# Output weights ahead of group 3, the first outputs inside the second tile, and 64-token blocks from group 3 on, in a fused attention and feed-forward kernel

## The chip, the cores and the metric

The kernel runs on one core of a Trainium2 chip. Its time is the device time of one execution in microseconds (us). An execution is called slow when it is over 1.5% above the fastest of its kernel in the same call; comparisons use the fast ones. "Clock" is the mean clock that TensorE was granted in an execution, as a share of full speed.

## The reference

Linear attention with a decay per head over 4 batches, 8 heads, 768 tokens and head size 64 gives x of 3072 x 512, and a gated feed-forward layer follows. The attention goes in blocks and carries a state:

```python
for b in range(nb):                                  # blocks of 64 tokens
    intra = einsum('bhic,bhjc->bhij', qb, kb) * Dmask    # within the block
    intra = einsum('bhij,bhjd->bhid', intra, vb)
    inter = einsum('bhid,bhde->bhie', qb * lam_pow, kv_state)
    out[:, :, sl] = intra + inter
    kv_state = lam_block * kv_state + einsum('bhsd,bhse->bhde', kb * rev_pow, vb)
# x = out, tokens in rows
g = x @ w_gate
out = (g * sigmoid(g) * (x @ w_val)) @ w_out         # 512 -> 1536 -> 512
```

## The kernel before

Twelve *groups* of attention (256 tokens of one batch each) feed six feed-forward *tiles* of 512 tokens, two groups to a tile. TensorE works through the tiles' steps; the attention of coming groups is put between steps by a plan. A tile has 12 steps (gate and value matmuls of 128 of the 1536 features) and 4 output blocks of 128 tokens. Tile 1 runs in half steps of 256 tokens, 12 for group 2's tokens and 12 for group 3's.

A group has this life: k, q, v are loaded; ScalarE casts k, VectorE scales q, GpSimd scales v; k and q are transposed (groups 0 to 2 on TensorE, from 3 on by a DMA); TensorE computes the state's updates and the scores; GpSimd adds the updates to the state; TensorE computes the state's part of the output, then the part within the block. Groups below `NAT0` go in blocks of 128 tokens, the others in blocks of 64 with smaller matmuls and more states:

```python
    NAT0 = 6
    def load_fp32(g, eng, src, what, h0=0, h1=H):
        ...
        if g < NAT0:                                   # one transfer, pieces of 2*D floats = 512 B
            eng.dma_start(out=t[:, h0:h1], in_=gsrc(src, g, h0)[:, 0:h1 - h0])
            return
        ...
        parts = [(0, 128, False)] if what == "v" else [(0, M, False), (M, M, True)]
        for s in range(2):                             # 2 transfers for v, 4 for k, 4 for q
            for p0, n, rev in parts:
                eng.dma_start(...)                     # pieces of D floats = 256 B

    def cast_scaled(g, eng=nc.vector):
        ...
        nc.scalar.copy(out=..., in_=...kraw...)        # k to bf16, ScalarE
        eng.tensor_tensor(out=..., in0=...qraw..., in1=qfac(g), op=ALU.mult)   # q, VectorE
        dma_transpose(g)                               # issued by SyncE

    def ahead(g):                                      # updates, state, scores
        upd(g); scores(g)

    def core_a(g):
        inter(g, True)                                 # the state's part
        guard(g)                                       # ScalarE reads one column, orders what follows

    def core_b(g, ...):
        run_later(len(later)); intra(g, False); evac(g, fns)

    def attend(g):                                     # one merged visit for g and g + 1
        core_a(g)
        upd_mm(g + 1); upd_copy(g + 1); scores(g + 1)
        core_b(g)
        state(g + 1)                                   # (cut: bounds and masks put off)
```

and the part of the plan in question (`s1a`, `s1b`: half steps of tile 1; `sn`: steps of tile t; `wo_cast`: the cast of one piece of the output weights, on GpSimd unless an engine is named, `ACTC` is ScalarE and `DVEC` VectorE):

```python
    at(s0[5], load_group, 3)
    at(s0["11b"], cast_scaled, 3, nc.gpsimd)
    ...
    at(s1a[3], cast_scaled, 4)
    at(s1a[3], load_group, 5)
    for c in range(0, FC, 2): at(s1a[3], wo_piece, c, c + 2)     # output weights, 3.1 MB
    ...                                                # group 3 in four visits, steps 7 to 10
    at(s1b[6], ahead, 4)
    at(s1b[8], wo_cast, ACTC)
    at(s1b[9], core_a, 4); at(s1b[10], core_b, 4)
    at(s1b[11], ...)                                   # 4 outputs of tile 0, group 5 between them
    # tile 2: outputs of tile 1 at steps 0, 3, 7, 9; ahead(6) at 2, attend(6) at 6, attend(7) at 10
```

Of the kernel before, what the change touches and what calls it, by code (L numbers as in the profile page):

```python
# [14 lines left out]
def bap(t: bass.AP, ap_dims, extra_offset=0) -> bass.AP:  # L15
    return bass.AP(tensor=t.tensor, offset=t.offset + extra_offset,
                   ap=[list(t.ap[0])] + [list(d) for d in ap_dims])
# [20 lines left out]
def _body(ctx, tc, nc, q, k, v, lam, moe_w_gate, moe_w_val, moe_w_out, out):  # L38
# [7 lines left out]
    FC = DFF // 128  # L46
# [6 lines left out]



    NAT0 = 6
    NB = 4
    PB = B // 2
    groups = [(t % PB * 2 + j, t // PB) for t in range(NG // 2) for j in range(2)]
# [25 lines left out]
    def gsrc(t, g, h0):  # L85
        b, i = groups[g]
        return bass.AP(tensor=t.tensor,
                       offset=t.offset + b * H * S * D + i * 2 * BLK * D + h0 * S * D,
                       ap=[[2 * D, 2 * M], [S * D, H - h0], [1, 2 * D]])

    st = {}

    def load_fp32(g, eng, src, what, h0=0, h1=H):
# [3 lines left out]
        t = st[(what, g)]  # L97
        if g < NAT0:
            eng.dma_start(out=t[:, h0:h1], in_=gsrc(src, g, h0)[:, 0:h1 - h0])  # L99
# [87 lines left out]
    def vfac(g, h0, h1):  # L187
        return bap(dec, [[8, h1 - h0], [1, 2], [0, D]], 8 * h0 + (0 if g < NAT0 else 4))

    def qfac(g):  # L190
        return bap(dec, [[8, H], [1, 2], [0, D]], 2) if g < NAT0 else bap(qdn, [[2, H], [1, 2], [0, D]])

# [116 lines left out]
    def scores(g, cs=(0, 1), warm=0):  # L309
        if g >= NAT0:  # L310
            scores_n(g)
# [55 lines left out]
    def upd_mm(g, up=None):  # L367
# [4 lines left out]
        for s in range(2):  # L372
            for hp in range(HP):
                for r in range(2):
                    if g >= NAT0 and i == NG // B - 1 and 2 * s + r == 3:
                        continue
                    for h2 in range(2):
                        ps = slice(r * M, r * M + M)
                        h = 2 * hp + h2
                        if g >= NAT0 and r:  # L380
                            h = H - 1 - h
# [9 lines left out]
    def upd_copy(g, parts=(0, 1)):  # L391
        b, i = groups[g]
        up = st[("up", g)]
        hd = "p (h d) -> p h d"
        if i == 0 and 0 in parts:
            kv = kv_pool.tile([128, HP, D], BF16, name="kvn", tag="kvn1", bufs=2)
            nc.scalar.copy(out=kv, in_=up[0][:, 0:HP * D].rearrange(hd, h=HP))
            st[("kv", g)] = [None, kv]
        if 1 not in parts:
            return  # L400
        src = []
        for r in range(2):
            n = HP * D if g < NAT0 or (r == 1 and i == NG // B - 1) else 2 * HP * D
            u = kv_pool.tile([128, 2 * HP * D], FP32, name="ups", tag="ups", bufs=4)
            nc.scalar.copy(out=u[:, 0:n], in_=up[r][:, 0:n])  # L405
            src += [(r, u, HP * D * j) for j in range(n // (HP * D))]

        st[("ups", g)] = [u[:, o:o + HP * D].rearrange(hd, h=HP)
                          for r, u, o in sorted(src, key=lambda x: (x[2], x[0]))]
# [29 lines left out]
    def phase(g, first, rs):  # L439
        hps = range(HP) if first else range(HP - 1, -1, -1)  # L440
        return [(hp, s, r, h2) for hp in hps for s in ((0, 1) if first else (1, 0))
                for h2 in range(2) for r in rs]
# [5 lines left out]
    def cols(g, hp, s):  # L448
        return slice((hp * 2 + s) * M, (hp * 2 + s) * M + M) if g >= NAT0 else slice(hp * BLK, hp * BLK + BLK)

    def inter(g, first):
        b, i = groups[g]
        tt, op = st[("qkt", g)], st[("op", g)]
        kv = st[("kv", g)] if ("kv", g) in st else [kv0[b][i % 2]]
        started = set()
        for hp, s, r, h2 in phase(g, first, (1,) if i == 0 else (0, 1) if first else (1, 0)):
            if g < NAT0 and s:
                continue
            n = 2 * s + r if g >= NAT0 else r
            row, hq = (1 - h2, HP - 1 - hp) if g >= NAT0 and r else (h2, hp)  # L460
            dp, rm = slice(row * 64, row * 64 + 64), slice(r * M, r * M + M)
            nc.tensor.matmul(op[r][h2 * 64:h2 * 64 + 64, cols(g, hp, s)], kv[n][dp, hp],  # L462
                             tt[dp, 1, s, hq, rm] if g >= NAT0 else tt[dp, 1, :, hp, rm],
                             start=(first and (r, h2) not in started), stop=(not first),
                             skip_group_check=True)
            started.add((r, h2))

    def intra(g, first):
        b, i = groups[g]
        op = st[("op", g)]  # L470
        ssb, v_s = st[("ssb", g)], st[("vs", g)]
        started = set()
        for hp, s, r, h2 in phase(g, first, (0, 1) if first else (1, 0)):
            ps = slice(r * M, r * M + M)
            nc.tensor.matmul(op[r][h2 * 64:h2 * 64 + 64, cols(g, hp, s)],  # L475
                             v_s[ps, 2 * hp + h2, s],
                             ssb[ps, h2, hp * 2 + s] if g >= NAT0 else ssb[ps, h2, hp, s],
                             start=((first or (i == 0 and r == 0)) and (r, h2) not in started),
                             stop=(not first), skip_group_check=True)
            started.add((r, h2))  # L480

# [14 lines left out]
    def core_b(g, fns=(nc.scalar.copy, nc.scalar.copy)):  # L496
        run_later(len(later))
        intra(g, False)
        evac(g, fns)
# [64 lines left out]
    ACTC, DVEC = nc.scalar.copy, nc.vector.tensor_copy  # L564
    SPLIT = (DVEC, ACTC)
# [37 lines left out]
    st[("op", 0)] = [bank() for _ in range(2)]  # L603
    warm_into(st[("op", 0)][0], 3)
    intra(0, True)
    ring[0] = 4
    guard(0)
# [21 lines left out]
    st[("op", 1)] = [bank() for _ in range(2)]  # L629
    warm_into(st[("op", 1)][0], 3)  # L630
    intra(1, True)
    guard(1)
    ring[0] = 2
# [20 lines left out]
    def step(t, fc, b0=0, b1=B):  # L654
        steps.append((t, fc, b0, b1))
        return len(steps) - 1

    def at(n, fn, *a):
        plan.setdefault(n, []).append((fn, a))

    s0 = {fc: step(0, fc) for fc in range(2, FC - 1)}
# [6 lines left out]
    at(s0[4], w_cast)  # L668
    at(s0[4], state, 1)
    at(s0[4], load_group, 2, "v")  # L670
    at(s0[5], load_group, 3)
    at(s0[6], w_cast)
    at(s0[7], load_group, 4, "kq")
    at(s0[7], cast_half, 2, 0, (ACTC, POOLC))
    at(s0[7], cast_half, 2, 1, (ACTC, POOLC))
    at(s0[8], pe_transpose, 2, 0)
# [5 lines left out]
    at(s0[10], upd_mm, 2)  # L682
    at(s0[10], upd_copy, 2)
    at(s0["11a"], core, 2, SPLIT)
    at(s0["11b"], cast_scaled, 3, nc.gpsimd)
    at(s0["11b"], v_scale, 3, nc.gpsimd)
    at(s0["11b"], state, 2)
    at(s0["11b"], load_group, 4, "v")

    s1a = [step(1, fc, 0, 2) for fc in range(FC)]  # L690
    s1b = [step(1, fc, 2, 4) for fc in range(FC)]
    at(s1a[3], cast_scaled, 4)
    at(s1a[3], load_group, 5)
    for c in range(0, FC, 2):
        at(s1a[3], wo_piece, c, c + 2)
    at(s1a[7], scores, 3, (0,))
    at(s1a[7], run_later, 2)
    at(s1a[8], scores, 3, (1,))
    at(s1a[8], upd_mm, 3)
    at(s1a[8], run_later, 2)  # L700
    at(s1a[8], upd_copy, 3)
    at(s1a[9], core_a, 3)
    at(s1a[10], core_b, 3, SPLIT)
    at(s1a[10], v_scale, 4, nc.gpsimd)
    at(s1a[10], state, 3)
    at(s1b[3], cast_scaled, 5)
    at(s1b[3], load_group, 6)
    at(s1b[4], wo_cast)
    at(s1b[4], wo_cast)
    at(s1b[6], ahead, 4)  # L710
    at(s1b[6], run_later, 2)
    at(s1b[6], wo_cast)
    at(s1b[6], wo_cast)
    at(s1b[6], v_scale, 5, nc.gpsimd)
    at(s1b[8], wo_cast, ACTC)
    at(s1b[8], wo_cast)
    at(s1b[9], core_a, 4)
    at(s1b[10], core_b, 4)
    at(s1b[11], ffn_out, 0, 0)
    at(s1b[11], ahead, 5)  # L720
    at(s1b[11], run_later, 3)
    at(s1b[11], ffn_out, 0, 1)
    at(s1b[11], core_a, 5)
    at(s1b[11], ffn_out, 0, 2)
    at(s1b[11], core_b, 5)
    at(s1b[11], cast_scaled, 6)
    at(s1b[11], load_group, 7)
    at(s1b[11], v_scale, 6, nc.gpsimd)
    at(s1b[11], ffn_out, 0, 3)

    outs = [(1, b) for b in range(4)]
    for t in range(2, NG // 2):
        sn = [step(t, fc) for fc in range(FC)]
        if t == 2:
            at(sn[2], ahead, 6)
        for j, g in ((3 if t == 2 else 0, 2 * t + 3), (7 if t == 2 else 6, 2 * t + 4)):
            if g < NG:
                at(sn[j], cast_scaled, g)
                if g + 1 < NG:
                    at(sn[j], load_group, g + 1)  # L740
                at(sn[1 + j], v_scale, g, nc.gpsimd)
        if t + 1 < NG // 2:
            at(sn[6 if t == 2 else 4], attend, 2 * t + 2)
            at(sn[10], attend, 2 * t + 3)
        for n, o in zip((0, 3, 7, 9), outs):
            at(sn[n], ffn_out, *o)
        outs = [(t, b) for b in range(4)]
# [41 lines left out]
```

## Time and profile before

| | before |
|---|---|
| time, median of 3 | 230.56 us (227.83 to 231.1) |
| profiled execution | span 227.1 us, clock 1.000 |
| TensorE busy | 218.5 us, 96% |
| ScalarE, VectorE, GpSimd busy | 47%, 40%, 39% |
| packets under 512 B | 57650 of 88012 |

The busy shares are averages over the span. For a program of stages they say which engine to look at; what a wait is worth has to be read from the stretch it lies in, so the prediction goes by timelines. In all timelines below a line is: start, length, engine, source line, operation, tile written <- tiles read, count, and in brackets the engine's idle time just before and what ended it.

### The profile page before, as it was taken

What the parts mean: (1) busy time and instruction counts of PE and PEld (TensorE: products, weight loads), DVE (VectorE), ACT (ScalarE), POOL (GpSimd) and SP (SyncE); (2) the same over time, 40 slices, a digit from 0 to 9 for tenths busy, and PEclk for the clock granted to TensorE, in tenths of its full rate; (3) what the DMA queues carried; (4) which work ended last, traced back from release to release, by engine and by line L of the source; (5) the groups of instructions that cost most, each with busy time, mean ns of one, the idle gap of its engine ahead of it and who ended that gap; (6) DMA issues with size and microseconds to landing.
All of it is one profiled execution on the core that took longest, in us unless ns stands there. A gap on an engine that the chain in (4) does not pass through costs nothing.

```text
span 227.1 us, 5890 instructions
## 1 busy us (share of the span) xinstructions
PE 218.5 (96%) x2432; PEld 118.2 (52%) x2444; DVE 90.1 (40%) x154; ACT 106.5 (47%) x209; POOL 88.2 (39%) x129
## 2 busy tenths in 40 slices
PE   7889999999979999999999999999999999999994
PEld 3556455878854444454544544544544444444443
DVE  2754357685825214545352362253242123222200
ACT  5868585754652446363454463453433423322221
POOL 6476736642793312978373092092150000000000
PEclk9999999999999999999999999999999999999999
DMA  6999999899997779799877748815101101101122
GB/s 199 345 360 377 367 354 313 210 255 352 300 219 189 206 168 222 177 200 191 217 178 186 185 98 214 214 36 139 49 3 48 46 3 46 46 0 46 49 92 92
DMA packets 88012, 39.70 MB, mean 175 GB/s; under 512 B 57650, under 2 KB 83506, under 8 KB 87986
## 3 DMA queue, kind: packets, MB, share of 16 engines
q1 hardware_dynamic: 83474, 32.64, 55.2%
q10 hardware_dynamic: 4512, 6.69, 8.3%
q8 instruction: 19, 0.31, 0.5%
q14 instruction: 7, 0.06, 0.1%
HBM read 28.31 MB, written 6.29 MB: 152 GB/s over the span
## 4 chain that ended last, share of the span: by engine, by line
PE 84%; DMA 6%; SPq 5%; issue 1%; DVE 1%; ACT 1%; DVEq 0%; ACTq 0%
PE bank L539 27%; PE bank L517 25%; PE bank L524 24%; DMA woraw<-in_moe_w_out_dram 4%; DMA qraw<-in_q_dram 2%; PE bank L475 2%; SPq L99 2%; SPq L228 2%; PE bank L462 2%; PE bank L383 1%; PE bank L353 1%; PE bank L327 1%; PE bank L290 1%; DVE ssb L334 1%; PE bank L168 0%
## 5 line engine op out<-in xcount | busy, mean ns | idle before, releaser
L527 DVE TENSOR_TENSOR h<-sil,bank 128x512 bf16<-128x512 bf16 (+1 forms) x87 | 51.4, 595 | 110.7 <-PE bank L524 94.5
L517 PE MATMUL bank<-xt,wg_sb 128*128 128x512 bf16 (+1 forms) x348 | 76.7, 343 | 0.0
L524 PE MATMUL bank<-xt,wv_sb 128*128 128x512 bf16 (+1 forms) x348 | 76.5, 342 | 0.0
L521 ACT ACTIVATE sil<-bank 128x512 bf16<-128x512 f32 (+1 forms) x87 | 45.8, 528 | 43.4 <-PE bank L517 40.4
L539 PE MATMUL bank<-wo_sb,h 128*128 128x512 bf16 (+1 forms) x288 | 64.2, 370 | 0.7 <-issue 0.2
L524 PEld LDWEIGHTS <-wv_sb 128*128 128x128 bf16 x348 | 34.0, 98 | 28.3
L517 PEld LDWEIGHTS <-wg_sb 128*128 128x128 bf16 x348 | 32.2, 98 | 27.4 <-DVE xt L487 0.5
L539 PEld LDWEIGHTS <-h 128*128 128x128 bf16 x300 | 29.1, 98 | 32.4
L541 ACT COPY osb<-bank 128x512 f32<-128x512 f32 (+1 forms) x24 | 13.8, 576 | 54.9 <-PE bank L539 52.9
L239 POOL TENSOR_TENSOR v_s<-v,dec 128x1024 bf16<-128x1024 f32 (+1 forms) x14 | 23.2, 1665 | 13.9 <-DMA v<-in_v_dram 9.5
L422 POOL TENSOR_TENSOR kvf<-kvs,ups 128x256 f32<-128x256 f32 x8 | 5.8, 726 | 45.1 <-ACT ups L405 40.1
L334 DVE TENSOR_TENSOR ssb<-bank,causal 128x512 bf16<-128x512 f32 x24 | 15.5, 684 | 3.9 <-PE bank L327 3.8
L487 ACT CAST xt<-bank 128x512 bf16<-128x512 f32 x21 | 12.8, 665 | 3.1 <-PE bank L475 2.3
L422 POOL TENSOR_TENSOR kvf<-kvf,ups 128x256 f32<-128x256 f32 x16 | 13.4, 839 | 0.6
L431 POOL CAST kvn<-kvf 64x256 bf16<-64x256 f32 x24 | 11.6, 483 | 1.5
L405 ACT COPY ups<-bank 128x256 f32<-128x256 f32 (+1 forms) x24 | 9.5, 450 | 2.3 <-PE bank L383 1.4
L259 ACT CAST qk<-kraw 128x1024 bf16<-128x1024 f32 x9 | 9.4, 1043 | 0.0
L261 DVE TENSOR_TENSOR qk<-qraw,qdn 128x1024 bf16<-128x1024 f32 x6 | 7.7, 1286 | 3.7 <-DMA qraw<-in_q_dram 3.7
L475 PE MATMUL bank<-ssb,v_s 64*64 64x128 bf16 (+1 forms) x384 | 7.2, 208 | 2.0 <-ACT guard L446 1.7
L222 POOL CAST wv_sb<-wraw 128x1024 bf16<-128x1024 f32 (+1 forms) x7 | 6.4, 918 | 6.1 <-DMA wraw<-in_moe_w_val_dram 6.0
L358 DVE TENSOR_TENSOR ssb<-bank,causaln 128x512 bf16<-128x512 f32 x12 | 8.3, 688 | 1.2 <-PE bank L353 1.1
L233 POOL CAST wo_sb<-woraw 128x1024 bf16<-128x1024 f32 x5 | 5.7, 1171 | 5.3 <-DMA woraw<-in_moe_w_out_dram 5.3
(62 smaller groups left out, 115.6 us busy)
## 6 DMA issues: line engine op xcount, KB each, us to landing
out_dram<-osb ACTq DMA_DIRECT2D x23, 256.0 KB, 2.5
v<-in_v_dram SPq DMA_DIRECT2D x16, 256.0 KB, 4.2
woraw<-in_moe_w_out_dram SPq DMA_DIRECT2D x6, 512.0 KB, 7.1
kraw<-in_k_dram SPq DMA_DIRECT2D x24, 128.0 KB, 3.2
qraw<-in_q_dram SPq DMA_DIRECT2D x24, 128.0 KB, 3.8
wraw<-in_moe_w_gate_dram SPq DMA_DIRECT2D x5, 512.0 KB, 6.6
wraw<-in_moe_w_val_dram SPq DMA_DIRECT2D x5, 512.0 KB, 7.3
kraw<-in_k_dram SPq DMA_DIRECT2D x4, 512.0 KB, 6.5
```

Of the source, the lines that this page charges most:

```text
L239: eng.tensor_tensor(out=st[("vs", g)][:, h0:h1], in0=st[("v", g)][:, h0:h1].rearrange("p h (s d) -> p h s d", s=2), in1=vfac(g, h0, h1), o ...
L334: nc.vector.tensor_tensor(out=ssb[:, h2, 2 * c:2 * c + 2].rearrange("p a s n -> p a (s n)"), in0=sp[(c, h2)].rearrange("p (a x) -> p a x", ...
L422: nc.gpsimd.tensor_tensor(out=o, in0=f, in1=u, op=ALU.add)
L431: nc.gpsimd.tensor_copy(out=o[64 - h2 * 64:128 - h2 * 64], in_=f[h2 * 64:h2 * 64 + 64])
L475: nc.tensor.matmul(op[r][h2 * 64:h2 * 64 + 64, cols(g, hp, s)], v_s[ps, 2 * hp + h2, s], ssb[ps, h2, hp * 2 + s] if g >= NAT0 else ssb[ps, ...
L487: fns[r](out=xt[:, g % 2, :, r].rearrange("p h (m s) -> p h s m", s=2) if g < NAT0 else xt[:, g % 2, :, :, r * M:r * M + M], in_=op[r].rea ...
L517: nc.tensor.matmul(gp[:, 0:N], wg_sb[:, mc, fs], xt[:, b0 // 2:b1 // 2, mc].rearrange("p g b n -> p g (b n)"), start=(mc == 0), stop=(mc = ...
L521: nc.scalar.activation(sil[:, 0:N], gp[:, 0:N], AF.Silu)
L524: nc.tensor.matmul(vp[:, 0:N], wv_sb[:, mc, fs], xt[:, b0 // 2:b1 // 2, mc].rearrange("p g b n -> p g (b n)"), start=(mc == 0), stop=(mc = ...
L527: nc.vector.tensor_tensor(out=h_sb[:, fc, b0:b1].rearrange("p b n -> p (b n)"), in0=sil[:, 0:N], in1=vp[:, 0:N], op=ALU.mult)
L539: nc.tensor.matmul(ps, h_sb[:, fc, b], wo_sb[:, fc, c0:c1], start=(fc == 0), stop=(fc == FC - 1))
L541: fn(out=osb[:, c0:c1], in_=ps)
```

## The change

Intent: take TensorE work out of groups 3 to 5 (fewer, merged visits in 64-token form), and have the output weights ready early, so that no cast of them holds up ScalarE.

```diff
-    NAT0 = 6
+    NAT0 = 3
...
-        if i == 0 and 0 in parts:
+        if i == 0 and g >= NAT0:
+            st[("kv", g)] = [None]
+        elif i == 0 and 0 in parts:
... (two further conditions of the same kind in inter and intra)
-    at(s0[5], load_group, 3)
+    for c in range(0, FC, 2):
+        at(s0[5], wo_piece, c, c + 2)
-    at(s0[7], load_group, 4, "kq")
+    at(s0[7], load_group, 3)
-    at(s0["11b"], cast_scaled, 3, nc.gpsimd)
-    at(s0["11b"], v_scale, 3, nc.gpsimd)
+    at(s0["11b"], wo_cast)
... (the other five casts of output weights at s1a[1] to s1a[6])
+    at(s1a[8], ffn_out, 0, 0)
+    at(s1a[8], cast_scaled, 3)
+    at(s1a[8], load_group, 4)
+    at(s1a[8], v_scale, 3, nc.gpsimd)
+    at(s1a[8], ffn_out, 0, 1)
+    at(s1a[8], ffn_out, 0, 2)
+    at(s1a[8], ahead, 3)
+    at(s1a[8], ffn_out, 0, 3)
+    at(s1a[10], core, 3, SPLIT)
+    at(s1a[11], cast_scaled, 4)
+    at(s1a[11], load_group, 5)
+    at(s1b[5], ahead, 4)
+    at(s1b[9], cast_scaled, 5)
+    at(s1b[9], load_group, 6)
+    at(s1b[11], ffn_out, 1, 0)
+    at(s1b[11], attend, 4)
+    at(s1b[11], ffn_out, 1, 1)
+    at(s1b[11], ffn_out, 1, 2)
+    at(s1b[11], cast_scaled, 6)
+    at(s1b[11], load_group, 7)
+    at(s1b[11], core, 5)
+    at(s1b[11], ffn_out, 1, 3)
-    outs = [(1, b) for b in range(4)]
+    outs = []
... (tile 2: ahead(6) at step 1, group 7's cast at 2, attend(6) at 5, one step earlier each)
```

## The prediction

> **What bounds the kernel now.** I read the page first: busy shares, then the chain that ended last.

> ```profile
> PE 218.5 (96%) x2432; PEld 118.2 (52%) x2444; DVE 90.1 (40%) x154; ACT 106.5 (47%) x209; POOL 88.2 (39%) x129
> PE 84%; DMA 6%; SPq 5%; issue 1%; DVE 1%; ACT 1%; DVEq 0%; ACTq 0%
> ```

> TensorE is the bound, so a change gains only by giving it less work or fewer waits. The feed-forward work is fixed: a step is eight 512-column matmuls, 1.73 us, an output tile twelve, 2.59 us; six tiles of 12 steps and 4 outputs are 6 x (20.7 + 10.4) = 187 us. Of 227 us, 15 are the start and 3 the end; the remaining 22 are attention and waits. So I went to TensorE's timeline around groups 3, 4 and 5, whose form changes. The number before the brackets is a count; the bracket is idle time before the piece. Here group 4:

> ```profile
> 59.48 0.45 PE L383 MATMUL bank<-v_s,qk 64*64 64x64 bf16 x32
> ...
> 64.08 0.60 PE L524 MATMUL bank<-xt,wv_sb 128*128 128x256 bf16 x4
> 65.88 0.64 PE L475 MATMUL bank<-ssb,v_s 64*64 64x128 bf16 x32 [1.21 <-ACT guard L446]
> 66.46 0.61 PE L517 MATMUL bank<-xt,wg_sb 128*128 128x256 bf16 x4
> ```

> The 1.21 us is the largest hole after the start. ScalarE's timeline explains it:

> ```profile
> 64.45 1.04 ACT L233 CAST wo_sb<-woraw 128x1024 bf16<-128x1024 f32 x1 [2.24 <-DMA woraw<-in_moe_w_out_dram]
> ```

> A cast of output weights waited for its transfer and everything behind it on ScalarE waited too. That is what the change wants to cure.

> Next, what else a 64-token group needs. The stretches view (per-engine busy time and instructions, then clock, DMA share, GB/s) and SyncE's and GpSimd's timelines for group 7, already in the new form:

> ```profile
> 93.20:105.40 12.20, 12.15 (x178) 6.12 (x177) 5.37 (x7) 6.69 (x13) 10.07 (x16) 1.00 0.95 195
> ```

> ```profile
> 93.18 2.00 SPq L252 DMA_TRANSPOSE qkt<-qk  x1
> 95.23 2.92 SPq L106 DMA_DIRECT2D kraw<-in_k_dram  x4
> 98.19 3.50 SPq L106 DMA_DIRECT2D qraw<-in_q_dram  x4
> 101.73 1.26 SPq L106 DMA_DIRECT2D v<-in_v_dram  x2
> 105.38 2.70 SPq L252 DMA_TRANSPOSE qkt<-qk  x1
> ```

> ```profile
> 103.91 1.33 DVE L261 TENSOR_TENSOR qk<-qraw,qdn 128x1024 bf16<-128x1024 f32 x1 [1.03 <-DMA qraw<-in_q_dram]
> ```

> ```profile
> 89.05 0.73 POOL L422 TENSOR_TENSOR kvf<-kvs,ups 128x256 f32<-128x256 f32 x1 [8.87 <-ACT ups L405]
> ...
> 91.92 1.70 POOL L422 TENSOR_TENSOR kvf<-kvf,ups 128x256 f32<-128x256 f32 x1
> ...
> 96.44 1.91 POOL L239 TENSOR_TENSOR v_s<-v,dec 128x1024 bf16<-128x1024 f32 x1
> ```

> Two chains run beside TensorE. **The transfer chain**: transpose of a group, then loading of the next, scaling, its transpose. From one transpose's issue (93.18) the next q landed at 103.91, 10.7 us; with 1.33 us scaling the period is 12.2 us, with the DMA engines 95% busy. v landed 14 us after the transpose issue (107.60 in GpSimd's timeline). **The GpSimd chain**: state update (89.05 to 96.44, 7.4 us) plus v scaling 1.91 us; with 1.2 us from the update matmuls (87.84) to its start, 10.5 us from one group's update matmuls to the next group's scaled v. Before, both chains just fit: group 7's scaled v is ready at 98.35, and its update matmuls start at 98.41.

> [...] The new form reads 64 values, 256 B, per piece, the old one 512 B. The trace agrees: 195 GB/s at 95% busy above, against 371 GB/s in the stretch from 20 to 30 us, whose pieces are 512 B and longer. [...] The trace agrees: the state addition that meets the q scaling (91.73 to 93.04) took 1.70 us, the others 0.72. [...]

> **The change, part by part.** Everything up to 40.4 us (first half-width step of tile 1) stays, apart from loads: the 3.1 MB of output weights now go ahead of group 3. In the before trace each 512 KB load there takes about 1.5 us of SyncE's queue; starting at 29 the last should land near 44 (an estimate), and its cast on GpSimd ends near 46. The outputs need it at 48.3. I expect no wait for weights.

> TensorE work, from 40.4 to the start of tile 3 (114.8 before; both kernels have done the same there, since tile 1's outputs move forward). Fixed: two tiles' steps and eight outputs, 62.2 us. Attention before: 74.4 - 62.2 = 12.2 us: group 3 in four visits 2.25, group 4 3.55 with its wait, group 5 2.3, groups 6 and 7 0.75 + 1.55 + 1.4, and about 0.4 of fringe. After, without waits: group 3 0.75 + 1.25, group 4's scores 0.75, the merged visit 1.4, group 5 alone about 1.0, groups 6 and 7 0.75 + 1.4 + 1.4: about 8.9. **Saving: 3.2 us**, 1.4%. That is all there is to win; the rest of the program is the same instructions.

> What it adds: group 3 is cast only at step 9 of tile 1 instead of at 40.5, behind the copy of the first output on ScalarE, and five groups (3 to 7) plus group 8's preparation must pass both chains before tile 3. Working along (us):
> - Outputs 48.3 to 50.9. ScalarE copies 0.6, issues the store 0.4, casts k 1.04: transpose 3 is issued at 53.1 and lands 4.3 later, 57.4 (shown: 3.7 to 5.5 uncongested). TensorE reaches the scores at 56.5: **wait 0.9**.
> - Output, two steps, group 3, seven half steps of 0.87: 69.5. Transpose 4 issued at 66.0, landed 70.3: **wait 0.3**.
> - Six half steps, an output, group 4's first part: 79.0. v of group 5 lands at 66.0 + 14 = 80, scaled 81.9; q at 76.7, transpose issued 78.1, landed 82.4. **Wait 3.4**, visit over at 83.3.
> - Two outputs: 88.5. Now the guard of group 5 stands on ScalarE behind an output copy, a store issue and k's cast, 2.1 us, while TensorE has 0.4 us of work: **wait 1.9**. Group 5 over 91.4, last output 94.0, two steps 97.5, group 6's update.
> - Four steps (6.9 us, no outputs between them any more; before there was one) and 0.4 lead to group 7's update at 105.5, but the GpSimd chain gives 97.6 + 10.5 = 108.1: **wait 2.6**.
> - Five steps: 117.9, group 8's v and transpose ready near 118.9: **wait 0.6**, end 119.8, last step 121.5.

> Waits 9.7 against 3.2 saved: **+6.5 us** in the straight working. [...]

> **Rivals.** (a) Transfers are quicker than in the before trace, as tile 2 has no stores beside them: period 11 us instead of 12.2, landing 3.7. Then the waits at groups 3, 5 and 8 shrink to about 0.4, 2.2 and 0, but guard and GpSimd waits stay: +3.5 us. For it: stores took about 12% of the queues' share between 82 and 106; against: 1.5 MB in 256 B pieces is most of the load either way. (b) The chains don't bite and the intent comes out: -3 us. For it: the hole at 64 is real and visits merge. Against: GpSimd's 10.5 us is a sum of durations no reordering shortens, and before it had no slack. (c) Output weights come late because 1.5 MB more is ahead of them than I think; ScalarE would block at its third cast near 43.9 and the steps behind it, as at 64.45 before: +2 on top. Against: 5 us of margin at that cast.

> **Range and chances.** The straight working gives +6.5, rival (a) +3.5, rival (b) -3. I weigh to +5.3. The three runs before average 229.8 us (227.8 to 231.1), so I predict 235.0 us. Eight in ten between 229.5 (rival (a) on a good run, or part of (b)) and 239.0 (with (c)). Faster by over 2% would need 4.6 us and only 3.2 can be saved: 0.03. Slower by over 2% needs +4.6, under the straight working and over (a): 0.58; within 2%: 0.39.

> **What would show it.** In the changed profile: TensorE busy falls under 95%; the waits list shows update and score matmuls or their weight loads held by scaled v (GpSimd) and by transposes in groups 5 and 7, and a hole of about 2 us before group 5's second part, released by the guard; transposes from group 3 on issued every 11 to 13 us; packets under 512 B up by some 18 thousand (three groups of 1.5 MB / 256 B), which makes DMA fuller between 45 and 115; the output-weight casts no longer wait 2 us; tile 3 begins near 120 instead of 114.8, and all after it only shifts. I am wrong if tile 3 begins at 112 to 114 with no holes in tile 2 (the chains have slack I don't see), or if the loss lies before 48 us.

## The result, and the profile after

| | before | after |
|---|---|---|
| time, median of 4 | 229.38 us (227.83 to 231.1) | 242.2 us (240.44 to 243.91) |
| ratio after / before | | 1.0556 (95%: 1.0436 to 1.0677) |
| profiled execution | 227.1 us, clock 1.000 | 240.3 us, clock 0.977 |
| tile 3 begins | 114.8 us | 128.1 us |

Ratios here and below are the mean time of one kernel's fast runs over that of the other's fast runs of the same rounds, so not quite the ratio of the medians. The change is 12.8 us slower. The direction was forecast, the size not: 242.2 lies above the range.

The page of the changed kernel, its busy shares, its chain that ended last, and the granted clock in 40 slices of the span (tenths of full speed):

```profile
PE 222.3 (93%) x2492; PEld 119.1 (50%) x2492; DVE 88.2 (37%) x149; ACT 108.5 (45%) x209; POOL 94.5 (39%) x146
PEclk9999999998899979799999999999999999999999
...
PE 69%; POOL 10%; DMA 9%; issue 5%; SPq 4%; DVE 1%; ACT 1%; POOLq 0%; DVEq 0%
```

TensorE's part of the chain has fallen from 84% to 69%; GpSimd, which did not appear before, has 10%. And the clock, at its full value throughout before (1.000), dips in three places (0.977 over the span).

TensorE's timeline of the changed kernel, the pieces that follow an idle time of over half a microsecond, and the outputs (source line 543) behind some of them:

```profile
58.28 0.45 PE L353 MATMUL bank<-qkt 64*64 64x64 bf16 x32 [1.72 <-DMA qkt<-qk]
58.66 4.45 PE L543 MATMUL bank<-wo_sb,h 128*128 128x512 bf16 x12
...
73.25 0.45 PE L353 MATMUL bank<-qkt 64*64 64x64 bf16 x32 [0.66 <-DMA qkt<-qk]
...
78.88 2.75 PE L543 MATMUL bank<-wo_sb,h 128*128 128x512 bf16 x12
...
84.03 0.45 PE L383 MATMUL bank<-v_s,qk 64*64 64x64 bf16 x32 [2.02 <-POOL v_s L239]
86.64 0.64 PE L353 MATMUL bank<-qkt 64*64 64x64 bf16 x32 [2.17 <-DMA qkt<-qk]
...
87.64 6.21 PE L543 MATMUL bank<-wo_sb,h 128*128 128x512 bf16 x24
...
96.12 0.58 PE L479 MATMUL bank<-ssb,v_s 64*64 64x64 bf16 x32 [1.89 <-ACT guard L448]
96.63 4.25 PE L543 MATMUL bank<-wo_sb,h 128*128 128x512 bf16 x12
...
114.90 0.44 PE L383 MATMUL bank<-v_s,qk 64*64 64x64 bf16 x32 [2.52 <-POOL v_s L239]
```

The waits stand where the prediction put them and end as it said: transposes (DMA qkt), scaled v (GpSimd), the guard. With 0.26 us at group 8 they sum to 11.2 us (11.5 with 0.30 us at group 3's guard); predicted were 9.7. Two of them can be read to the tenth: the guard 1.89 (predicted 1.9) and group 7's updates 2.52 (2.6).

But look at the outputs: twelve matmuls of 512 columns take 2.75 us at 78.88, and 4.25 us from 96.63 on. The stretches view of the changed kernel (length, busy us and instructions of PE, PEld, DVE, ACT, POOL, then the granted clock, DMA share and GB/s), cut at the clock's changes:

```profile
55.24:58.65 3.41, 1.70 (x69) 0.88 (x67) 0.00 (x0) 1.66 (x3) 0.58 (x2) 1.00 0.88 219
58.65:62.06 3.41, 3.41 (x20) 1.18 (x10) 1.29 (x2) 0.00 (x0) 3.06 (x7) 0.51 1.06 269
82.50:85.90 3.40, 0.45 (x32) 0.33 (x31) 0.00 (x0) 1.23 (x3) 2.15 (x2) 1.00 1.00 241
85.90:89.30 3.40, 2.66 (x68) 1.52 (x69) 1.29 (x2) 1.07 (x2) 3.04 (x7) 0.52 0.71 158
```

Each pair is a stretch with a wait in it and the stretch after it: TensorE was busy 1.70 and 0.45 us of some 3.4, and for the next 3.4 us it had half its clock. A third such stretch begins at 96.3, after one with 1.5 us busy. The three together cost 1.7 + 0.9 + 1.5 = about 4.0 us: the lengths 4.45, 6.21 and 4.25 us of the outputs in them, less the 2.76, 5.35 and 2.76 us that the same outputs take at full clock in the filler run below. The prediction has no such term.

SyncE's timeline, the transposes of groups 3, 4 and 8:

```profile
53.21 1.73 SPq L252 DMA_TRANSPOSE qkt<-qk  x1
...
69.35 1.60 SPq L252 DMA_TRANSPOSE qkt<-qk  x1
...
121.92 1.61 SPq L252 DMA_TRANSPOSE qkt<-qk  x1
```

Those of groups 5, 6 and 7, cut here, are issued at 81.73, 96.03 and 109.66.

Before, the transposes of groups 3, 4 and 5 were issued at 41.6, 45.9 and 58.7, those of 6, 7 and 8 at 80.2, 93.2 and 105.4. The changed kernel starts this chain 12 us later and has not caught up at group 8, 16.5 us behind. And what was to be cured is cured. ScalarE's timeline has no wait left at its casts of output weights:

```profile
43.93 1.04 ACT L233 CAST wo_sb<-woraw 128x1024 bf16<-128x1024 f32 x1
...
45.68 1.04 ACT L233 CAST wo_sb<-woraw 128x1024 bf16<-128x1024 f32 x1
```

From tile 3 on both kernels do the same. So all of the loss arises between 40 and 128 us.

### The profile page after: what moved, and what is told of

It reads as the page before. It is cut to its first block, busy times and chain, and to the rows that moved or that the text cites. A ratio compares the mean times of both kernels' runs of the same rounds, so it can differ in the third digit from the quotient of the medians.

```text
span 240.3 us, 6057 instructions
## 1 busy us (share of the span) xinstructions
PE 222.3 (93%) x2492; PEld 119.1 (50%) x2492; DVE 88.2 (37%) x149; ACT 108.5 (45%) x209; POOL 94.5 (39%) x146
## 3 DMA queue, kind: packets, MB, share of 16 engines
q1 hardware_dynamic: 93026, 32.65, 53.1%
q10 hardware_dynamic: 4512, 6.69, 7.7%
## 4 chain that ended last, share of the span: by engine, by line
PE 69%; POOL 10%; DMA 9%; issue 5%; SPq 4%; DVE 1%; ACT 1%; POOLq 0%; DVEq 0%
PE bank L521 21%; PE bank L528 21%; PE bank L543 20%; POOL kvf L424 4%; DMA v<-in_v_dram 4%; POOL v_s L239 3%; SPq L106 2%; DMA qraw<-in_q_dram 2%; DMA qkt<-qk 2%; POOL kvn L433 2%; PE bank L479 2%; PE bank L383 1%; PE bank L466 1%; SPq L99 1%; DMA out_dram<-osb 1%
## 5 line engine op out<-in xcount | busy, mean ns | idle before, releaser
L521 PE MATMUL bank<-xt,wg_sb 128*128 128x512 bf16 (+1 forms) x348 | 76.7, 343 | 0.0
L543 PE MATMUL bank<-wo_sb,h 128*128 128x512 bf16 (+1 forms) x300 | 69.2, 387 | 0.0
L543 PEld LDWEIGHTS <-h 128*128 128x128 bf16 x300 | 30.1, 101 | 35.1 <-issue 5.3
L239 POOL TENSOR_TENSOR v_s<-v,dec 128x1024 bf16<-128x1024 f32 (+1 forms) x14 | 23.2, 1666 | 21.5 <-DMA v<-in_v_dram 18.6
L358 DVE TENSOR_TENSOR ssb<-bank,causaln 128x512 bf16<-128x512 f32 x18 | 12.2, 687 | 19.0 <-PE bank L353 18.8
L424 POOL TENSOR_TENSOR kvf<-kvf,ups 128x256 f32<-128x256 f32 x22 | 17.9, 815 | 1.1
L433 POOL CAST kvn<-kvf 64x256 bf16<-64x256 f32 x34 | 15.6, 458 | 2.1
L261 DVE TENSOR_TENSOR qk<-qraw,qdn 128x1024 bf16<-128x1024 f32 x9 | 11.6, 1286 | 9.0 <-DMA qraw<-in_q_dram 8.8
L407 ACT COPY ups<-bank 128x512 f32<-128x512 f32 (+1 forms) x24 | 10.8, 503 | 7.1 <-PE bank L383 6.2
L383 PE MATMUL bank<-v_s,qk 64*64 64x64 bf16 x352 | 5.3, 195 | 4.8 <-POOL v_s L239 4.8
L479 PE MATMUL bank<-ssb,v_s 64*64 64x64 bf16 (+1 forms) x384 | 6.8, 208 | 2.9 <-ACT guard L448 2.7
L353 PE MATMUL bank<-qkt 64*64 64x64 bf16 x288 | 4.6, 200 | 4.5 <-DMA qkt<-qk 4.5
```

The source lines that it names most:

```text
L239: eng.tensor_tensor(out=st[("vs", g)][:, h0:h1], in0=st[("v", g)][:, h0:h1].rearrange("p h (s d) -> p h s d", s=2), in1=vfac(g, h0, h1), o ...
L358: nc.vector.tensor_tensor(out=ssb[:, h2], in0=sp[h2].rearrange("p (a x) -> p a x", x=M), in1=bap(causaln, [[0, 2 * HP], [1, M]]), op=ALU.mult)
L424: nc.gpsimd.tensor_tensor(out=o, in0=f, in1=u, op=ALU.add)
L433: nc.gpsimd.tensor_copy(out=o[64 - h2 * 64:128 - h2 * 64], in_=f[h2 * 64:h2 * 64 + 64])
L479: nc.tensor.matmul(op[r][h2 * 64:h2 * 64 + 64, cols(g, hp, s)], v_s[ps, 2 * hp + h2, s], ssb[ps, h2, hp * 2 + s] if g >= NAT0 else ssb[ps, ...
L521: nc.tensor.matmul(gp[:, 0:N], wg_sb[:, mc, fs], xt[:, b0 // 2:b1 // 2, mc].rearrange("p g b n -> p g (b n)"), start=(mc == 0), stop=(mc = ...
```

## The experiments

My theory after the result: two chains beside TensorE (transfers, and GpSimd's state updates) are too slow for a start of group 3 at 53 us, and the waits they cause bring half clock on top. Rivals: the 64-token form alone is to blame; the late start alone; or the half clock comes from something else than the waits.

The runs under one heading below were made in one call, on one chip, and share the executions of before; different calls went to different chips, so differences between them are less certain than the ratios to before.

### One part at a time (one call; before 229.29 us)

**Form only**: groups 3 to 5 in 64-token form on the schedule of before.

```diff
-    NAT0 = 6
+    NAT0 = 3
... (with the three conditions of the change)
-    ... group 3 in four visits at s1a[7] to s1a[10]
+    at(s1a[7], ahead, 3)
+    at(s1a[11], core, 3, SPLIT)
```

> Groups 3 to 5 in the 64-token form on the schedule of before (output weights late, first tile's outputs late, group 3 cast early; group 3's four visits become two, as its state must precede it). Theory (the form itself lengthens the transfer and GpSimd chains): 3 to 9 us slower than before, 232 to 238 us, with new waits for k, q and v loads between 43 and 80 us. Rival (only the late start of group 3 costs): equal to before or up to 3 us faster, 226 to 230 us.

Measured: 245.12 us (ratio 1.0715), slower than the whole change. The rival falls, and the theory was too mild by 7 us. TensorE's and GpSimd's timelines show why:

```profile
70.68 0.26 PE L466 MATMUL bank<-qkt,kvn 64*64 64x64 bf16 x1 [2.62 <-POOL kvn L433]
```

```profile
65.87 1.04 POOL L233 CAST wo_sb<-woraw 128x1024 bf16<-128x1024 f32 x1 [7.50 <-DMA woraw<-in_moe_w_out_dram]
68.44 1.04 POOL L233 CAST wo_sb<-woraw 128x1024 bf16<-128x1024 f32 x1 [1.53 <-DMA woraw<-in_moe_w_out_dram]
```

With more transfer time ahead of them the output weights are issued at 60.8 us instead of 50.2 and land late, GpSimd stands 7.5 and 1.5 us at their casts, and group 4's state update behind them makes TensorE wait. The granted clock was 0.965. The changed order of the output weights spares the new form these waits; no run changes that order alone.

**Schedule only**: the changed kernel with groups 3 to 5 back in 128-token form.

```diff
-    NAT0 = 3
+    NAT0 = 6
-    at(s1a[8], run_later, 2)
+    at(s1a[8], run_later, 3)          # four masks instead of two; the same at s1b[11]
```

> The changed kernel with groups 3 to 5 back in 128-token blocks of 512-byte pieces. Theory (form and late start both cost): the waits at groups 4 and 5 (0.7 and 4.2 us) vanish, those at group 3 (1.7), the guard (1.9) and group 7 (2.5) stay, so 232 to 237 us. Rival A (the form alone costs): 230 us or less. Rival B (the late start alone costs): 240 us or more, with group 5's waits still there.

Measured: 239.07 us, the median of four executions of which one is slow (240.97); the three fast ones have a median of 237.68 (ratio 1.0416), 0.7 us above the range given, between theory and rival B. Group 5's wait for v is gone, as the theory had it, so rival B in its strict form falls; but group 4's did not vanish (1.23 us), and the guard and GpSimd waits are all there:

```profile
93.32 0.64 PE L479 MATMUL bank<-ssb,v_s 64*64 64x128 bf16 x32 [1.70 <-ACT guard L448]
...
110.66 0.64 PE L383 MATMUL bank<-v_s,qk 64*64 64x64 bf16 x32 [2.50 <-POOL v_s L239]
```

Each part alone loses, 7.2% and 4.2% by the ratios, and the two together 5.6%. So their losses don't add; that both wait for the same transfers is how I read it, not a separate test.

### The guard and the clock (same call)

**Guard first**: group 5's second part ahead of group 6's casts.

```diff
-    at(s1b[11], cast_scaled, 6)
-    at(s1b[11], load_group, 7)
-    at(s1b[11], v_scale, 6, nc.gpsimd)
     at(s1b[11], core, 5)
+    at(s1b[11], cast_scaled, 6)
+    at(s1b[11], load_group, 7)
+    at(s1b[11], v_scale, 6, nc.gpsimd)
```

> The changed kernel with group 5's second part issued ahead of group 6's casts, so that the guard copy on ScalarE no longer stands behind k's cast. Theory (a wait costs its own length and then a stretch of half clock): the 1.9 us wait goes and the slow output after it runs at full clock, 3 to 3.5 us off, 238.5 to 239.5 us. Rival A (the low clock has another cause): 1.9 us off and the output still slow, 240.3. Rival B (the chains take it back): the wait at group 7 or 8 grows by as much, 241.5 to 242.5.

Measured: 240.33 us, 240.09 without its one slow execution (1.0493). The wait at the guard fell from 1.89 to 0.87 us, not to nothing: an output copy and a store's issue still stand ahead of it. The output after it ran at full speed (2.76 us). The wait at group 7's updates was 2.82 us, against 2.52: 0.3 us came back behind the edit, as rival B says. (Group 5's updates and scores, 3.01 and 0.94 us against 2.02 and 2.17, stand ahead of it.) This profile, of clock 0.979, has three half-clock stretches too, after the waits of groups 5 and 7, none of them after the guard. The interval is too wide to tell 1.9 from 3 us in time, so the run doesn't decide between theory and rivals.

**Filler**: dummy matmuls put at six places (the expectation counts five waits).

```diff
         sp = [bank() for _ in range(2)]
+        warm_into(sp[0], {3: 12, 4: 4, 5: 15}.get(g, 0))     # scores
...
         up = up or [bank() for _ in range(2)]
+        warm_into(up[0], {5: 14, 7: 18}.get(g, 0))           # updates
...
+        if g == 5:
+            warm_into(banks[ring[0] % 8], 13)                # second part
         intra(g, False)
```

> The changed kernel with dummy matmuls of 256 columns in five of its waits (12 before group 3's scores, 4 before group 4's, 14 and 15 before group 5's updates and scores, 13 before group 5's second part, 18 before group 7's updates), sized to end before the waited-for data comes. Theory (idle TensorE brings the half clock): the waited-for data comes at the same times, the granted clock is 0.995 or above, 4 to 5 us off, 237 to 238.5 us. Rival (the low clock has another cause, such as the dense outputs themselves): clock still about 0.98 and 241 us or more.

Measured: 239.38 us (1.0462; 238.98 to 239.69). Granted clock 1.000, 1.000, 1.000 and 0.998 in four executions, against 0.971 to 0.986 for the changed kernel. The same stretches as above, now with TensorE kept busy:

```profile
55.50:58.65 3.15, 2.88 (x81) 1.91 (x79) 0.00 (x0) 1.66 (x3) 0.60 (x2) 1.00 0.90 222
58.65:62.06 3.41, 3.41 (x24) 1.92 (x21) 1.29 (x2) 0.59 (x1) 3.06 (x7) 1.00 1.05 267
82.00:85.95 3.95, 2.98 (x112) 2.46 (x112) 0.30 (x1) 1.07 (x2) 2.49 (x5) 1.00 1.01 194
85.95:89.36 3.41, 3.41 (x17) 1.53 (x16) 0.99 (x2) 1.66 (x3) 3.06 (x7) 1.00 0.84 188
```

That settles the clock: matmuls whose results nobody reads, in the waits, remove the half clock (1.00 behind both waits, where the changed kernel had 0.51 and 0.52), so here it is the idle TensorE that brings it. The rival falls. But the time fell by 2.8 us against the changed kernel's first median (242.2) and by 1.0 against a later one (240.36, below), not by the 4 to 5 expected. The reason is in the wait before group 8's scores, which is now 1.23 us:

```profile
122.73 0.45 PE L354 MATMUL bank<-qkt 64*64 64x64 bf16 x32 [1.23 <-DMA qkt<-qk]
```

TensorE arrives earlier and waits for the transfer chain. In this run the chain is not stretched by a slow TensorE, and it still takes from 53.19 to 119.03 us for the transposes of groups 3 to 8, 13.2 us each on average. The first interval, 13.8 us, is set by the place of group 4's cast in the plan (its scaling at 65.65 waits for no load); in the other four, 13.0 us each, the scaling of q waits for its load.

### The two chains (one call; before 228.77 us)

**Early chain**: the guard-first kernel with the casts of groups 3, 4 and 5 moved up.

```diff
-    at(s1a[8], ffn_out, 0, 0)
     at(s1a[8], cast_scaled, 3)
     at(s1a[8], load_group, 4)
     at(s1a[8], v_scale, 3, nc.gpsimd)
+    at(s1a[8], ffn_out, 0, 0)
... (group 4's cast, load and v scaling from s1a[11] to s1a[9], group 5's from s1b[9] to s1b[8])
```

> The kernel of the guard-first run (240.3 us) with casts and transposes of groups 3, 4 and 5 issued earlier: group 3's ahead of the first output instead of behind it (about 3 us), group 4's two half steps earlier, group 5's one. No matmul changes place. Theory (the chain transpose, next load, scaling, transpose sets the waits): each transpose from group 3 to group 8 is issued about 3 us earlier and the time falls by 2 to 4 us, 236.5 to 238.5 us. Rival (GpSimd's state updates set the waits): transposes come earlier but the updates of groups 5 and 7 still wait for scaled v, 239.5 us or more.

Measured: 235.12 us (1.0287, interval 1.0238 to 1.0335), 5.2 us better than guard first by the medians and 4.7 by the ratios to before, more than expected. SyncE's timeline, transposes of groups 3 and 8:

```profile
50.25 2.16 SPq L252 DMA_TRANSPOSE qkt<-qk  x1
...
113.96 1.60 SPq L252 DMA_TRANSPOSE qkt<-qk  x1
```

In the guard-first run these were 52.96 and 119.87. The first comes 2.7 us earlier, the last 5.9. Not one matmul was taken out or moved. The place of a cast on ScalarE and VectorE, far off the chain of matmuls, is worth 2% here. Part of that is the clock: the profile has no half-clock stretch (clock 1.000), guard first has three (0.979). And the rival is not gone: group 5's and 7's updates still wait 1.52 and 2.15 us for scaled v.

**v on VectorE**: the filler kernel with group 7's v scaled on VectorE, and without the dummies there.

```diff
-                at(sn[1 + j], v_scale, g, nc.gpsimd)
+                at(sn[1 + j + (g == 7)], v_scale, g, nc.vector if g == 7 else nc.gpsimd)
```

> The filler kernel (239.4 us) without its 18 dummies at group 7, and with group 7's v scaled on VectorE instead of GpSimd, so that it no longer stands behind group 6's state update. Theory (two chains side by side; behind GpSimd's the transfer chain waits): the wait at group 7's updates, 2.5 us, goes to under 0.7 us, but the wait at group 8's transpose grows by about as much, and the time moves by under 1 us, 238.5 to 240 us. Rival (GpSimd's chain alone binds in tile 2): 2 us off, 237.4 us.

Measured: 239.67 us (1.0494), against 239.38 for the filler. TensorE's timeline at groups 7 and 8:

```profile
109.67 0.44 PE L385 MATMUL bank<-v_s,qk 64*64 64x64 bf16 x32 [0.49 <-DVE v_s L239]
110.77 0.45 PE L354 MATMUL bank<-qkt 64*64 64x64 bf16 x32 [0.66 <-DMA qkt<-qk]
...
122.05 0.44 PE L385 MATMUL bank<-v_s,qk 64*64 64x64 bf16 x24 [1.43 <-POOL v_s L239]
123.54 0.45 PE L354 MATMUL bank<-qkt 64*64 64x64 bf16 x32 [1.05 <-DMA qkt<-qk]
```

The wait of 2.5 us (in the filler 0.28 us behind 2.14 us of dummies) shrank to 0.49 us and the time did not fall; 0.66 us appeared right behind it, and group 8 waits 2.5 us where the filler had 0.38 and 1.23. What grew there is not the wait for the transpose, as expected, but the one for scaled v; SyncE's timeline has the load of that v issued from 114.82 to 117.07 us, in the filler from 113.56 to 114.85, so I put it down to the transfer chain all the same. The rival falls: a wait that can be removed with no effect is the sign of a second chain of about the same length beside the first.

### Size of the pieces (one call with the next two; before 228.35 us)

**Big pieces**: the changed kernel, wrong on purpose. Groups 3 to 5 are loaded in 512-byte pieces as before, but computed in the 64-token form.

```diff
     def load_fp32(g, eng, src, what, h0=0, h1=H):
         ...
-        if g < NAT0:
+        if g < 6:
```

> The changed kernel (242.2 us), wrong on purpose: groups 3 to 5 are loaded in 512-byte pieces, one transfer each for k, q and v as in before, and computed as if they lay in the 64-token order; matmuls, GpSimd's work and all places are those of the changed kernel. Theory (the small pieces lengthen the transfer chain): loads of groups 4 and 5 land 4 us or more earlier, the transposes of groups 5 to 8 are issued 3 to 5 us earlier, the waits at group 5 fall from 4.2 to under 2 us, 236.5 to 239 us. Rival (group 3's late cast and GpSimd alone set the waits): no change, 241 us or more.

Measured: 237.18 us (1.0385, interval 1.0339 to 1.0432), its output wrong as intended, against 240.36 us for the changed kernel in the same call (1.052, 1.0487 to 1.0554): 3.2 us. The waits at group 5's updates and scores are 0.20 and 0.57 us, for 2.00 and 2.35 in the changed kernel's profile of this call, and the transpose of group 8 is issued at 116.25 for 120.73 (that of group 5 only 1.2 us earlier, less than expected). The rival falls. Of the 3.2 us up to 1.7 can be the clock: this profile has one half-clock stretch (clock 0.993), that of the changed kernel two (0.984). In SyncE's queue the loads of group 5 take 2.6 us in all (69.81 to 72.40); in 256-byte pieces, in the changed kernel's first profile, they took 7.0 us (71.47 to 78.45). Pieces and number of transfers (three for ten) change together here; which of the two counts, the run does not separate.

**The changed kernel again.**

> The changed kernel once more, for the spread of its clock: theory (each stretch of half clock costs about 1.7 us of full-clock work and whether a wait brings one on is chance): times from 238.5 to 244 us that fall as the mean granted clock rises, about 1.7 us for each 0.007 of clock. Rival: no relation of time and clock.

Measured: 240.36 us (240.05 to 240.71, six executions), clock 0.984 to 0.986 in all. The spread that I wanted to use was not there, so this run does not test the relation. It gives the changed kernel a second median; the difference of 1.8 us to the first call remains, and part of it goes with clocks of 0.971 and 0.977 seen only there.

**One hole**: the best version below with a wait put far from all chains.

```diff
+    def hole():
+        t = const.tile([128, 512], BF16, name="hole")
+        for _ in range(4):
+            nc.scalar.copy(out=t, in_=warm)
+        nc.tensor.matmul(banks[ring[0] % 8][:, 0:128], t[:, 0:128], t[:, 0:128], start=True, stop=True)
+    ... (after step 9 of tile 4)
```

> The merged-visit version of before (227.7 us) with one wait put into tile 4, far from all chains: after step 9 TensorE waits for four copies on ScalarE, some 2 us. Theory (a wait costs its length, and in part of the executions a stretch of half clock on top): executions with clock 1.000 come out 1.5 to 2.5 us slower than without, and some, between a tenth and a half of them, another 1.5 us or so slower with clock near 0.993. Rival (waits never lower the clock by themselves): all executions 1.5 to 2.5 us slower at clock 0.997 or above.

Measured: 231.8 us (1.0147). One of six executions had clock 1.000 and took 230.41 us; five had 0.990 to 0.993 and took 231.43 to 232.97, on average 232.1. The profiled one shows the hole and the two stretches around it:

```profile
175.54 0.23 PE L748 MATMUL bank<-hole 128*128 128x128 bf16 x1 [2.47 <-ACT hole L747]
```

```profile
172.50:175.90 3.40, 0.93 (x6) 0.32 (x5) 0.69 (x1) 2.89 (x5) 0.00 (x0) 1.00 0.21 80
175.98:179.38 3.40, 3.40 (x10) 1.18 (x8) 0.41 (x1) 0.60 (x1) 0.00 (x0) 0.50 0.00 0
```

### What would help instead (same call as the early chain)

**Hole fix**: the kernel before with only the intended cure.

```diff
-    at(s1b[8], wo_cast, ACTC)
-    at(s1b[8], wo_cast)
     at(s1b[10], core_b, 4)
+    at(s1b[10], wo_cast, ACTC)
+    at(s1b[10], wo_cast, DVEC)
```

> The kernel before with only the intended cure: the last two casts of output weights are moved from step 9 of tile 1's second half (one on ScalarE, one on GpSimd) to behind group 4's second part, on ScalarE and VectorE. Theory (the hole of 1.2 us at 64 us is worth its length, as TensorE binds): 1 to 1.5 us faster, 0.4 to 0.7 per cent, and the hole gone. Rival (the output matmuls then wait for the weights instead): same time, with the wait in the first output.

Measured: 228.08 us over 22 executions, before 228.77 over 40; ratio 0.998, interval 0.9955 to 1.0005. The wait at ScalarE's cast is gone; in the profiled execution 0.20 us stand at the VectorE cast and 0.49 us at group 5's transpose instead. The expected gain of 1 us or more did not come: inconclusive between the two.

**Hole fix and one visit less**: the same, and group 3's scores and updates in one visit.

```diff
-    at(s1a[7], scores, 3, (0,))
... (scores, upd_mm, upd_copy of group 3 at s1a[7] and s1a[8], state at s1a[10])
+    at(s1a[8], ahead, 3)
```

> The same, and group 3's scores and updates in one visit instead of two, in the old form. Theory (a visit costs about 0.1 to 0.2 us of TensorE beyond its matmuls): another 0.2 to 0.4 us off. Rival: within noise of the run before it.

Measured: 227.74 us over 18 executions, ratio 0.9964, interval 0.9942 to 0.9985. It is the only version that beats before, by 0.4%, far inside the 2% that counts as the same here. A second thing shows in the lists of executions: of the 40 of before, six are slow, 231.5 to 233.9 us, and each of these has clock 0.993 or 0.983; of the 40 of these two versions none is below 0.997. (One of the 22 hole-fix executions is slow too, 230.74 us, at clock 0.999.) Whether the hole of 1.2 us at 64 us brings those on is not shown. In the profile of before, the emptiest 3.41 us after the start, around that hole, still have TensorE busy for 2.16 us, more than the 1.82 that were followed by full clock in the changed kernel; the profiled execution was a fast one.

## Why the prediction was wrong

By its own steps:

- *Bound and saving*: the bound right, the saving somewhat large. TensorE's time outside waits, half clock and fixed work from 40.3 us to tile 3 was about 10 us, predicted 8.9, so some 2 us of attention were saved and not 3.2. (The terms of the 8.9 add to 8.7, and 12.2 - 8.9 is 3.3; small slips.)
- *No wait for output weights*: right; outputs began at 48.25 (predicted 48.3).
- *GpSimd chain of 10.5 us*: right. Group 6's updates began at 104.26, group 7's v was scaled at 114.85: 10.6 us. The wait was 2.52, predicted 2.6.
- *Guard*: right, 1.89 for 1.9.
- *Rivals (a), quicker transfers, and (b), no waits*: wrong, and they pulled the forecast from +6.5 to +5.3, the wrong way. (By its own waits, rival (a) comes to about +4, not +3.5.)
- *Transfer chain with a period of 12.2 us*: the mechanism right, the term too small. The transposes landed 3.7 to 5.2 us after their issue in the changed kernel, 3.7 to 5.5 before (and once 10.5, behind 3.1 MB of output weights). The filler run, in which TensorE has full clock, has 13.0 us in the four intervals that the loads set, and the transpose of group 8 at 119.0 where the working had 114.6. The 12.2 came from one period of the kernel before (its neighbours were 13.0 and 13.6), with 10.7 us from the transpose's issue to the next scaling of q; in the filler run these were 11.9, 11.4, 11.2 and 11.7 us. That makes 3.5 of the 4.4 us; the other 0.9 are in the first interval, which the place of group 4's cast sets.
- *"Waits 9.7 against 3.2 saved"*: here is the step that failed in kind. Each wait was charged its length and nothing else. The waits summed to 11.2 us, near enough (with luck in the parts: 1.72 for 0.9 at group 3, 4.2 for 3.4 at group 5, 0.26 for 0.6 at group 8), but three of them were followed by 3.4 us at half clock, which cost 4.0 us in the profiled execution. By the filler run the net worth of that is 1.0 to 2.8 us in the medians and 3.0 in the profiled executions (240.3 and 237.3), because TensorE at full clock meets the transfer chain.

Together: tile 3 was predicted at 121.5 and began at 128.1. At full clock (filler) it begins at 125.1, so by this comparison 3.6 us of the 6.6 belong to the transfer chain, at whose last transpose the filler run waits, and 3.0 to the clock. The forecast signs also held: packets under 512 B rose by 18768 (18 thousand predicted), TensorE busy 93% (under 95%). The spacing of transposes, "11 to 13 us", was 12.3 to 16.1.

What cost the time in the end, by the experiments: the chain's late start (moving the casts up by a few microseconds gave back 4.7 to 5.2 us), the small pieces in many transfers (3.2), and idle time turned into half clock (1.0 to 2.8). These overlap, as the first two contain some of the third, and must not be added.

## What to carry to other kernels

When work is moved to another place for TensorE's sake, ask first what else hangs on that place: here a cast that starts a chain of transfers was moved 12 us back, and five later groups each needed 13 us of that chain. A chain that just fits (before, scaled v came 0.06 us ahead of its use) has a price for any delay, and shortening one of two parallel chains of about the same length gained nothing here (v on VectorE). Charge a wait of TensorE of about two microseconds not only with its length but with the possible half clock after it: in the changed kernel it came after stretches of 3.4 us in which TensorE was busy for 0.45 to 1.70 us, and in the one-hole run after one with 0.93 us. Dummy matmuls in the wait are a quick test of how much that is (here the clock went from 0.971 to 0.986 up to 0.998 to 1.000).
